# A convolution by matmul transforms beside a gated MLP: block-diagonal transforms of 128 rows replaced by pairs of dense 64-row matmul tiles

## The chip, the cores and the metric

One core of one Trainium2 chip runs the whole program. The metric is device time in microseconds (us) for one execution. Times quoted are medians of several executions. Most executions of one kernel agree within about 1%. Engine names in the profile: PE is TensorE (matmuls), PEld its weight loads, DVE is VectorE, ACT is ScalarE, SP issues the transfers (DMA).

## The reference, cut to what matters

Three parts are added: the input, a long convolution of a gated sequence done through a Fourier transform, and a gated MLP ("gate/up" and "down" below). Inputs have 2048 positions and 640 channels, the MLP has 1728 hidden columns, all in bf16.

```python
def reference(A_q, A_k, A_v, A_shift_k, A_ssm_k, A_ssm_D, B_x, B_w_gate, B_w_up, B_w_down):
    def _A_ref(q, k, v, shift_k, ssm_k, ssm_D):
        B, S, D = q.shape
        ks = shift_k.shape[-1]
        k_pad = jnp.pad(k, ((0, 0), (ks - 1, 0), (0, 0)))
        k_shift = jnp.zeros_like(k)
        for t in range(ks):
            k_shift = k_shift + k_pad[:, t:t + S, :] * shift_k[:, ks - 1 - t][None, None, :]
        kv = k_shift * v
        L = 2 * S
        kv_pad = jnp.pad(kv, ((0, 0), (0, S), (0, 0)))
        kf_pad = jnp.pad(ssm_k, ((0, 0), (0, S)))
        kv_f = (lambda x, axes=(-2,-1): jnp.fft.rfft2(x.astype(jnp.float32), axes=axes))(kv_pad[:, None, :, :], axes=(1, 2))
        kf_f = (lambda x, axes=(-2,-1): jnp.fft.rfft2(x.astype(jnp.float32), axes=axes))(kf_pad[:, None, :], axes=(1, 2))
        kf_f = (lambda x, *d: x.transpose(*d))(kf_f, 1, 2, 0)
        y_f = kv_f * kf_f[None, :, :, :]
        y = (lambda x, s, axes=(-2,-1): jnp.fft.irfft2(x, s=s, axes=axes).astype(jnp.bfloat16))(y_f, (1, L), axes=(1, 2))[:, 0, :S, :]
        y = y + kv * ssm_D[None, None, :]
        return q * y

    def _B_ref(x, w_gate, w_up, w_down):
        g = jnp.einsum("bsd,df->bsf", x, w_gate)
        u = jnp.einsum("bsd,df->bsf", x, w_up)
        h = _sigmoid(g) * u
        return jnp.einsum("bsf,fd->bsd", h, w_down)

    x = A_q
    xn = _layernorm(x, axis=-1)
    return x + _A_ref(xn, A_k, A_v, A_shift_k, A_ssm_k, A_ssm_D) + _B_ref(xn, B_w_gate, B_w_up, B_w_down)
```

## The kernel before

The kernel does the transforms as matmuls. 640 channels are cut into 10 steps of 64. Each step goes through:

- the first transform (`rec_st1`): data is the stationary operand, the table `F` moves; the result T goes to SBUF by ScalarE;
- the second transform (`rec_st2`): table `M` is stationary, T moves; the result is the spectrum S (real and imaginary part, of the gated sequence and of the filter);
- the complex product on VectorE (`rec_prod`) gives Z;
- the third and fourth transform go back.

The tables of the first two are block-diagonal: 128 rows hold two independent problems of 64 rows, so half of what TensorE multiplies is zero. (The third's table is padded in the same way.) ScalarE builds the padded table `Mb` from a dense one at the start (`load_M`).

All operations are recorded with priorities and planned durations; a small list scheduler inside the program then fixes the order of instructions on each engine. Gate/up and down matmuls fill TensorE between the steps of the convolution. The constants `GA, GB, CA, CB` set those priorities. Tags such as "c" and "g" are buffer pools: "c" has 3 PSUM banks for transforms, "g" has 5 for the MLP.

```python
    def load_M(pri):
        b = "Mc"

        def view():
            return tl[b][:, 0:K1 * 2 * K2].bitcast(F16).rearrange("p (k s m) -> p k s m", s=2, m=K2)
        for i in range(2):
            ks = slice(16 * i, 16 * i + 16)
            dma(lambda ks=ks: nc.sync.dma_start(view()[:, ks].bitcast(U16), Mdram.ap()[:, ks]), 512, 4096,
                w=[(b, i)], alloc=[(b, "V")] if i == 0 else (), pri=pri)
        for i in range(4):
            ks = slice(8 * i, 8 * i + 8)
            for p in range(2):
                cs = slice(p * K2, (p + 1) * K2)
                m, mn = Wm[:, p:p + 1], Wm[:, 2 + p:3 + p]
                act(1024 + 200, lambda ks=ks, cs=cs, m=m: nc.scalar.activation(
                    Mb[:, ks, 0:2, cs], view()[:, ks], ACT.Copy, scale=m),
                    r=[(b, i // 2), ("W",)], w=[("M", i, p, 0)], pri=pri + 24)
                act(512 + 200, lambda ks=ks, cs=cs, mn=mn: nc.scalar.activation(
                    Mb[:, ks, 2, cs], view()[:, ks, 1], ACT.Copy, scale=mn),
                    r=[(b, i // 2), ("W",)], w=[("M", i, p, 1)], pri=pri + 24)

    # ... (loads, shift and gating of k and v)

    def rec_st1(idx, pri, dp):
        half, sub = divmod(idx, NSUB)
        j0 = sub * JS
        part = 0 if j0 < HPART[0][1] else 1
        hb = f"ht{half}{part}"
        hj = j0 - HPART[part][0]
        hr = [(hb, g, p) for g in range(G) for p in range(2)]
        T = f"T{idx}"
        for j in range(JS):
            c = f"c1_{idx}_{j}"

            def f(j=j, c=c):
                pt = tl[c].rearrange("p (x n) -> p x n", x=2)
                nc.tensor.matmul(pt[:, 0, :], lhsT=tl[f"kvt{idx}"][:, :, :, j].rearrange("p b n -> p (b n)"),
                                 rhs=Fb[:], start=True, stop=True)
                nc.tensor.matmul(pt[:, 1, :], lhsT=tl[hb][:, hj + j, :, :].rearrange("p b n -> p (b n)"),
                                 rhs=Fb[:], start=True, stop=True)
            pe(2 * mm(256), f, r=[(f"kvt{idx}",), ("F",)] + hr + ([(T, "a")] if j else []),
               w=[(c,)] + ([] if j else [(T, "a")]), alloc=[(c, "c")] + ([] if j else [(T, "T")]), pri=pri + dp * j / JS)
            act(512, lambda j=j, c=c: nc.scalar.copy(out=tl[T][:, :, j, :],
                                                     in_=tl[c].rearrange("p (x n) -> p x n", x=2)),
                r=[(c,)], w=[(T, j)], pri=pri + dp * j / JS)

    def rec_st2(idx, pri, dp):
        T, S_ = f"T{idx}", f"S{idx}"
        for kb8 in range(K1 // 8):
            for im in range(2):
                c = f"c2_{idx}_{kb8}_{im}"

                def f(kb8=kb8, im=im, c=c):
                    Tv = tl[T].rearrange("p x j (k r g) -> p (x j) k r g", r=2, g=G)
                    pp = tl[c].rearrange("p (k n) -> p k n", k=8)
                    for kk in range(8):
                        k = 8 * kb8 + kk
                        nc.tensor.matmul(pp[:, kk, :], lhsT=Mb[:, k, 0, :], rhs=Tv[:, :, k, im, :],
                                         start=True, stop=False)
                        nc.tensor.matmul(pp[:, kk, :], lhsT=Mb[:, k, 1 + im, :], rhs=Tv[:, :, k, 1 - im, :],
                                         start=False, stop=True)

                def ev(kb8=kb8, im=im, c=c):
                    dst = tl[S_][:, im].rearrange("p x (j k g) -> p k x j g", k=K1, g=G)
                    for_in = tl[c].rearrange("p (k x g) -> p k x g", k=8, g=G)
                    nc.scalar.copy(out=dst.rearrange("p k x j g -> p k (x j) g")[:, 8 * kb8:8 * kb8 + 8], in_=for_in)
                q = pri + dp * (2 * kb8 + im) / 8
                z = (kb8, im) == (0, 0)
                pe(16 * mm(64), f, r=[(T, j) for j in range(JS)] + ([] if z else [(S_, "a")]) +
                   [("M", kb8, p, e) for p in range(2) for e in range(2)],
                   w=[(c,)] + ([(S_, "a")] if z else []), alloc=[(c, "c")] + ([(S_, "S")] if z else []), pri=q)
                act(512, ev, r=[(c,)], w=[(S_, im)], pri=q)

    def rec_prod(idx, pri):
        S_, Z = f"S{idx}", f"Z{idx}"
        n = JS * K1 * G

        def X(im):
            return tl[S_][:, im, 0, :]

        def H(im):
            return tl[S_][:, im, 1, :]

        def tv(b):
            return tl[b].rearrange("p n b j -> p (n b j)")

        sr = [(S_, 0), (S_, 1)]
        for o, (a, b, cc, d, al) in enumerate(((0, 0, 1, 1, ALU.subtract), (0, 1, 1, 0, ALU.add))):
            t = f"tp{idx}_{o}"
            dve(n, 2, lambda o=o, a=a, b=b: nc.vector.tensor_tensor(tl[Z][:, o], X(a), H(b), ALU.mult),
                r=sr, w=[(Z, o)], alloc=[(Z, "Z")] if o == 0 else (), pri=pri)
            dve(n, 2, lambda t=t, cc=cc, d=d: nc.vector.tensor_tensor(tv(t), X(cc), H(d), ALU.mult),
                r=sr, w=[(t,)], alloc=[(t, "t")], pri=pri)
            dve(n, 2, lambda t=t, o=o, al=al: nc.vector.tensor_tensor(tl[Z][:, o], tl[Z][:, o], tv(t), al),
                r=[(t,)], w=[(Z, o)], pri=pri)
```

## Time and profile before

| | before |
|---|---|
| median of 3 runs, us | 303.77 (302.59 to 306.47) |
| span of the profiled execution, us | 300.3 |
| PE / DVE / ACT busy | 93% / 63% / 59% |
| second transform: matmuls, distance of starts | 1280 of 64 columns, 29 ns |
| first transform: matmuls, distance of starts | 160 of 256 columns, 109 ns |

The first lines of the page of the kernel before. In the slices each digit is one fortieth of the span, in tenths busy; PEclk is the granted TensorE clock in tenths.

```profile
span 300.3 us, 7199 instructions
...
PE 278.7 (93%) x2957; PEld 184.7 (62%) x2957; DVE 188.6 (63%) x414; ACT 176.4 (59%) x364; POOL 0.7 (0%) x6
...
PE   8793999799999599999999999999998999999993
...
ACT  1551289979898398768467678796964534510000
...
PEclk9998699999999999999999999999999999999998
```

PE is nearly full over most of the span. Its largest holes are at the left, and PEclk drops (6) just after the deepest.

Two windows of the kernel before; the columns are busy us of PE, PEld, DVE, ACT and POOL, then granted clock, DMA share and GB/s.

```profile
20.00:40.00 20.00, 14.86 (x67) 6.47 (x66) 8.67 (x15) 6.27 (x11) 0.00 (x0) 0.83 1.04 170
40.00:60.00 20.00, 17.72 (x87) 8.48 (x85) 19.59 (x52) 19.46 (x31) 0.00 (x0) 1.00 1.03 285
```

Between 40 and 60 us ACT is busy 19.5 of 20 us, and PE only 17.7. The weight loads of the second transform, in the groups of instructions (count, busy us, mean ns):

```profile
L531 PEld LDWEIGHTS <-Mb 128*128 128x128 f16 x640 | 40.5, 97 | 1.9
...
L412 ACT ACTIVATE Mb<-V_389,Wm 128x1024 f16<-128x1024 f16 x8 | 9.2, 1148 | 0.0
...
L415 ACT ACTIVATE Mb<-V_389,Wm 128x512 f16<-128x512 f16 x8 | 5.8, 722 | 0.0
```

The table takes ACT 9.2 + 5.8 = 15.0 us. The second transform, in order of time; the columns are start, duration, engine, line:

```profile
61.66 0.38 PE L689 MATMUL g_669<-xnT_177,w_601 128*128 128x512 bf16 x1
...
61.88 0.19 PE L531 MATMUL c_678<-T_530,Mb 128*128 128x64 bf16 x1
61.88 0.10 PEld L533 LDWEIGHTS <-Mb 128*128 128x128 f16 x1
61.91 0.19 PE L533 MATMUL c_678<-T_530,Mb 128*128 128x64 bf16 x1
...
61.94 0.19 PE L531 MATMUL c_678<-T_530,Mb 128*128 128x64 bf16 x1
...
61.97 0.20 PE L533 MATMUL c_678<-T_530,Mb 128*128 128x64 bf16 x1
```

The matmuls start 29 to 30 ns apart, though each lasts 190 ns: they are pipelined, so busy time per matmul says little and the distance of starts is what counts. Each has its own weight load of about 97 ns, which also runs at that pace. The first matmul of the group follows the last gate/up matmul after 0.22 us, which is just that matmul's own 512 columns. So TensorE is the bound, and the second transform fills 1280 x 29 ns = 37 us of it, the first 160 x 109 ns = 17.5 us.

What TensorE waited for, longest first (the list of waits; total us, times, longest):

```profile
PE c_356 L445 <- DMA kt_164<-in_A_k_dram: 5.1, 1, 5.1
PE g_1473 L689 <- DMA w_1324<-in_B_w_up_dram: 3.2, 1, 3.2
...
PE c_3920 L586 <- DVE Z_3879 L567: 1.2, 1, 1.2
```

### The profile page before, as it was taken

To read this page: it belongs to the slowest core of one execution; us is meant where nothing else is said; L and a number is where in the kernel's file an instruction comes from. 1 tells how busy PE (TensorE), PEld (TensorE's weight loads), DVE (VectorE), ACT (ScalarE), POOL (GpSimd) and SP (SyncE) were. 2 spreads that over 40 slices of the span, in tenths; PEclk is the share of its full clock that TensorE was granted. 3 is DMA by queue.
4 is the path that set the end of the run, shared out by engine and by line. 5 is a ranking of instruction groups with operands and counts; after the bars stand their busy time and mean duration, and the time that the engine had idled before them with its cause. 6 is when DMAs were issued, how large, how long until landed. Compare 5 with 4: busy or idle time off the path is not lost.

```text
span 300.3 us, 7199 instructions
## 1 busy us (share of the span) xinstructions
PE 278.7 (93%) x2957; PEld 184.7 (62%) x2957; DVE 188.6 (63%) x414; ACT 176.4 (59%) x364; POOL 0.7 (0%) x6
## 2 busy tenths in 40 slices
PE   8793999799999599999999999999998999999993
PEld 3351345376767287887787786667664545567772
DVE  6971599999965599978325244433599372236531
ACT  1551289979898398768467678796964534510000
POOL 0000000000000000000000000000000000000000
PEclk9998699999999999999999999999999999999998
DMA  7899899933599900850388604871909499659411
GB/s 231 223 155 139 154 315 370 183 35 75 114 148 148 201 2 3 127 156 2 106 203 207 122 0 78 156 203 41 160 24 196 130 267 262 140 101 203 169 46 44
DMA packets 135688, 42.33 MB, mean 141 GB/s; under 512 B 109736, under 2 KB 131304, under 8 KB 135656
## 3 DMA queue, kind: packets, MB, share of 16 engines
q1 hardware_dynamic: 135656, 41.88, 66.2%
q8 instruction: 23, 0.38, 0.6%
q14 instruction: 9, 0.07, 0.1%
HBM read 36.62 MB, written 5.24 MB: 139 GB/s over the span
## 4 chain that ended last, share of the span: by engine, by line
PE 61%; DVE 13%; DMA 13%; SPq 8%; issue 3%; ACT 0%; DVEq 0%; ACTq 0%
SPq L442 3%; DMA kt_164<-in_A_k_dram 2%; DMA At<-dftA 2%; DMA w_1324<-in_B_w_up_dram 2%; SPq L743 2%; SPq L440 2%; DMA kt_3465<-in_A_q_dram 2%; DMA B_2337<-dftB 1%; DMA B_4063<-dftB 1%; DMA yd<-yt_2464 1%; DMA B_2695<-dftB 1%; DVE kt_3465 L748 1%; DVE hT_83 L704 1%; DVE st_540 L645 1%; DVE hT_82 L704 1%
## 5 line engine op out<-in xcount | busy, mean ns | idle before, releaser
L531 PEld LDWEIGHTS <-Mb 128*128 128x128 f16 x640 | 40.5, 97 | 1.9
L533 PEld LDWEIGHTS <-Mb 128*128 128x128 f16 x640 | 39.3, 97 | 1.9
L717 PEld LDWEIGHTS <-hT_82 128*128 128x128 bf16 x224 | 21.5, 98 | 7.8
L717 PEld LDWEIGHTS <-hT_83 128*128 128x128 bf16 x224 | 21.4, 98 | 7.6
L779 PE MATMUL g_89<-sig_85,ident 128*128 128x512 bf16 x31 | 8.4, 439 | 1.4 <-POOL ident masks.py:199 1.4
L412 ACT ACTIVATE Mb<-V_389,Wm 128x1024 f16<-128x1024 f16 x8 | 9.2, 1148 | 0.0
L689 PEld LDWEIGHTS <-w_97 128*128 128x128 bf16 x40 | 4.3, 109 | 6.8 <-issue 3.5
L689 PEld LDWEIGHTS <-w_427 128*128 128x128 bf16 x40 | 3.9, 97 | 5.8 <-issue 2.0
L779 PEld LDWEIGHTS <-ident 128*128 128x128 bf16 x31 | 3.4, 111 | 5.9 <-issue 2.1
L689 PEld LDWEIGHTS <-w_401 128*128 128x128 bf16 x40 | 3.8, 98 | 5.1 <-DMA w_401<-in_B_w_up_dram 0.5
L689 PEld LDWEIGHTS <-w_158 128*128 128x128 bf16 x40 | 3.9, 100 | 4.6 <-issue 0.6
L689 PEld LDWEIGHTS <-w_1324 128*128 128x128 bf16 x30 | 2.7, 97 | 6.3 <-DMA w_1324<-in_B_w_up_dram 3.7
L563 DVE TENSOR_TENSOR Z_2985<-S_2763 128x1024 bf16<-128x1024 bf16 x2 | 1.4, 688 | 8.2 <-ACT S_2763 L539 8.2
L689 PEld LDWEIGHTS <-w_3845 128*128 128x128 bf16 x40 | 3.7, 98 | 4.0
L689 PEld LDWEIGHTS <-w_3556 128*128 128x128 bf16 x40 | 3.8, 98 | 3.8
L672 ACT COPY xnT_177<-g_176 128x640 bf16<-128x640 bf16 x1 | 0.7, 693 | 8.9 <-PE g_176 L669 8.9
L689 PEld LDWEIGHTS <-w_4034 128*128 128x128 bf16 x40 | 3.6, 98 | 3.5
L415 ACT ACTIVATE Mb<-V_389,Wm 128x512 f16<-128x512 f16 x8 | 5.8, 722 | 0.0
L689 PEld LDWEIGHTS <-w_935 128*128 128x128 bf16 x40 | 3.8, 98 | 3.0
L689 PEld LDWEIGHTS <-w_601 128*128 128x128 bf16 x40 | 3.7, 97 | 3.2
L689 PEld LDWEIGHTS <-w_2088 128*128 128x128 bf16 x40 | 3.7, 98 | 2.9
L689 PEld LDWEIGHTS <-w_3268 128*128 128x128 bf16 x40 | 3.6, 97 | 2.9
(1275 smaller groups left out, 918.5 us busy)
## 6 DMA issues: line engine op xcount, KB each, us to landing
out_dram<-acc SPq DMA_DIRECT2D x8, 320.0 KB, 2.6
acc<-in_A_q_dram SPq DMA_DIRECT2D x3, 640.0 KB, 6.3
wd<-in_B_w_down_dram SPq DMA_DIRECT2D x3, 480.0 KB, 7.8
kt_164<-in_A_k_dram SPq DMA_DIRECT2D x4, 320.0 KB, 7.2
vt_170<-in_A_v_dram SPq DMA_DIRECT2D x4, 320.0 KB, 7.2
kt_1144<-in_A_k_dram SPq DMA_DIRECT2D x4, 320.0 KB, 7.1
vt_1231<-in_A_v_dram SPq DMA_DIRECT2D x4, 320.0 KB, 7.6
vt_3066<-yd SPq DMA_DIRECT2D x16, 80.0 KB, 2.7
```

Source lines behind the costliest of these rows:

```text
L412: act(1024 + 200, lambda ks=ks, cs=cs, m=m: nc.scalar.activation(Mb[:, ks, 0:2, cs], view()[:, ks], ACT.Copy, scale=m), r=[(b, i // 2), (" ...
L415: act(512 + 200, lambda ks=ks, cs=cs, mn=mn: nc.scalar.activation(Mb[:, ks, 2, cs], view()[:, ks, 1], ACT.Copy, scale=mn), r=[(b, i // 2), ...
L440: dma(lambda c0=c0, r0=r0: nc.sync.dma_start(ktv(half)[r0:r0 + N1, 3:3 + N2, :], k3[:, :, c0:c0 + HALF]), 320, 160, w=[(kb, g)], alloc=[(k ...
L442: dma(lambda c0=c0, r0=r0: nc.sync.dma_start(vtv(half)[r0:r0 + N1, :, :], v3[:, :, c0:c0 + HALF]), 320, 160, w=[(vb, g)], alloc=[(vb, "vt" ...
L531: nc.tensor.matmul(pp[:, kk, :], lhsT=Mb[:, k, 0, :], rhs=Tv[:, :, k, im, :], start=True, stop=False)
L533: nc.tensor.matmul(pp[:, kk, :], lhsT=Mb[:, k, 1 + im, :], rhs=Tv[:, :, k, 1 - im, :], start=False, stop=True)
L645: dve(320, 1, lambda i=i, s2=s2: nc.vector.bn_stats(stat(i, s2), acc[:, 4 * tr + i, s2 * 320:(s2 + 1) * 320]), r=[("acc", 4 * tr + i)], w= ...
L689: nc.tensor.matmul(tl[c][:], lhsT=tl[wb][:, k, o:o + P], rhs=tl[X][:, k, :], start=(k == 0), stop=(k == NC - 1))
L704: dve(512, 1, lambda c=c: nc.vector.tensor_tensor(hT[:, fc, :], tl[sg][:], tl[c][:], ALU.mult), r=[(c,), (sg,)], w=[(hk, fc)], pri=pri)
L717: nc.tensor.matmul(tl[pd[i]][:, 0:320], lhsT=hT[:, fc, t4 * P:(t4 + 1) * P], rhs=wd[:, fc, 320 * i:320 * i + 320], start=(fc == 0), stop=( ...
L743: dma(lambda qs=qs, g=g: nc.sync.dma_start(xv()[:, qs, g, :], xs[:, g, qs, cs]), 160, 160, w=[(xb, j) for j in range(8 * i, 8 * i + 8)], a ...
L779: plan.op("PE", 0.3, lambda: nc.tensor.matmul(tl["wps"][:], lhsT=ident[:], rhs=tl["warm"][:], start=True, stop=True), r=[("warm",)], w=[(" ...
```

## The change

The intent is to stop multiplying zeros. A 64-row matmul uses the upper or the lower half of the array's rows. The idea is that two of them, on different halves, run side by side. So:

- `F` and `M` become dense. Every full-row matmul of the first two transforms becomes a pair of 64-row ones, each with half the useful width, into separate PSUM banks;
- the second transform puts the real part on partitions 0 to 63 and the imaginary part on 64 to 127. The product then needs S with its halves exchanged: two transfers of 256 KB per step do that. In exchange the product is two VectorE operations of 2048 elements in place of six of 1024. Its additions do not vanish: they move into the third transform, whose table loses its zeros and takes the signs (320 matmuls of 128 columns in place of 160 of 256, the same columns in all);
- the dense `M` is loaded whole (1.5 MB instead of 1 MB) and ScalarE no longer builds a table;
- the pools become 4 and 4 banks, as pairs need them, and the scheduler's constants were set anew.

```diff
# the tables
-    M = np.zeros((2, N2, K1, 2, K2))
-    M[:, :, :, 0, :] = np.cos(th)[None]
-    M[:, :, :, 1, :] = np.sin(th)[None]
-    M = M.reshape(P, K1, 2, K2)
+    M = np.zeros((2, N2, K1, 3, K2))
+    M[:, :, :, 0, :] = np.sin(th)[None]
+    M[:, :, :, 1, :] = np.cos(th)[None]
+    M[:, :, :, 2, :] = -np.sin(th)[None]
+    M = M.reshape(P, K1, 3 * K2)
# ... (the first table likewise for two groups of channels; masks removed)
# sizes and constants
-    GA, GB = 25.0, 125.0
-    CA, CB = 35.0, 205.0
+    GA, GB = 25.0, 140.0
+    CA, CB = 35.0, 215.0
-   ... "c": 3, "g": 5}
+   ... "c": 4, "g": 4}
# ... (load_M: 16 ScalarE operations removed, table loaded dense, 1.5 MB)
+    def mm2(i, out, lhs, rhs, start, stop):
+        for h in range(2):
+            rs = slice(64 * h, 64 * h + 64)
+            nc.tensor.matmul(out[h], lhsT=lhs[rs], rhs=rhs[rs], start=start, stop=stop)
+
# rec_st1
-        for j in range(JS):
-            c = f"c1_{idx}_{j}"
-
-            def f(j=j, c=c):
-                pt = tl[c].rearrange("p (x n) -> p x n", x=2)
-                nc.tensor.matmul(pt[:, 0, :], lhsT=tl[f"kvt{idx}"][:, :, :, j].rearrange("p b n -> p (b n)"),
-                                 rhs=Fb[:], start=True, stop=True)
-                nc.tensor.matmul(pt[:, 1, :], lhsT=tl[hb][:, hj + j, :, :].rearrange("p b n -> p (b n)"),
-                                 rhs=Fb[:], start=True, stop=True)
-            pe(2 * mm(256), f, r=[(f"kvt{idx}",), ("F",)] + hr + ([(T, "a")] if j else []),
-               w=[(c,)] + ([] if j else [(T, "a")]), alloc=[(c, "c")] + ([] if j else [(T, "T")]), pri=pri + dp * j / JS)
-            act(512, lambda j=j, c=c: nc.scalar.copy(out=tl[T][:, :, j, :],
-                                                     in_=tl[c].rearrange("p (x n) -> p x n", x=2)),
-                r=[(c,)], w=[(T, j)], pri=pri + dp * j / JS)
+        for u in range(2 * JS // 4):
+            x, jq = u % 2, 4 * (u // 2)
+            cs = [f"c1_{idx}_{u}_{h}" for h in range(2)]
+
+            def f(x=x, jq=jq, cs=cs):
+                pt = [tl[c].rearrange("p (j n) -> p j n", j=4) for c in cs]
+                for j in range(4):
+                    if x == 0:
+                        lhs = tl[f"kvt{idx}"][:, :, :, jq + j].rearrange("p b n -> p (b n)")
+                    else:
+                        lhs = tl[hb][:, hj + jq + j, :, :].rearrange("p b n -> p (b n)")
+                    mm2(j, [q[:, j, :] for q in pt], lhs, Fb, True, True)
+            q = pri + dp * u / 4
+            pe(4 * mm(128), f, r=[("F",)] + ([(f"kvt{idx}",)] if x == 0 else hr) + ([(T, "a")] if u else []),
+               w=[(c,) for c in cs] + ([] if u else [(T, "a")]),
+               alloc=[(c, "c") for c in cs] + ([] if u else [(T, "T")]), pri=q)
+            for h in range(2):
+                act(512, lambda x=x, jq=jq, h=h, c=cs[h]: nc.scalar.copy(
+                    out=tl[T][:, x, jq:jq + 4, :, 2 * h:2 * h + 2],
+                    in_=tl[c].rearrange("p (j k g) -> p j k g", j=4, g=2)),
+                    r=[(cs[h],)], w=[(T, u, h)], pri=q)
 
     def rec_st2(idx, pri, dp):
         T, S_ = f"T{idx}", f"S{idx}"
         for kb8 in range(K1 // 8):
-            for im in range(2):
-                c = f"c2_{idx}_{kb8}_{im}"
-
-                def f(kb8=kb8, im=im, c=c):
-                    Tv = tl[T].rearrange("p x j (k r g) -> p (x j) k r g", r=2, g=G)
-                    pp = tl[c].rearrange("p (k n) -> p k n", k=8)
-                    for kk in range(8):
-                        k = 8 * kb8 + kk
-                        nc.tensor.matmul(pp[:, kk, :], lhsT=Mb[:, k, 0, :], rhs=Tv[:, :, k, im, :],
-                                         start=True, stop=False)
-                        nc.tensor.matmul(pp[:, kk, :], lhsT=Mb[:, k, 1 + im, :], rhs=Tv[:, :, k, 1 - im, :],
-                                         start=False, stop=True)
-
-                def ev(kb8=kb8, im=im, c=c):
-                    dst = tl[S_][:, im].rearrange("p x (j k g) -> p k x j g", k=K1, g=G)
-                    for_in = tl[c].rearrange("p (k x g) -> p k x g", k=8, g=G)
-                    nc.scalar.copy(out=dst.rearrange("p k x j g -> p k (x j) g")[:, 8 * kb8:8 * kb8 + 8], in_=for_in)
-                q = pri + dp * (2 * kb8 + im) / 8
-                z = (kb8, im) == (0, 0)
-                pe(16 * mm(64), f, r=[(T, j) for j in range(JS)] + ([] if z else [(S_, "a")]) +
-                   [("M", kb8, p, e) for p in range(2) for e in range(2)],
-                   w=[(c,)] + ([(S_, "a")] if z else []), alloc=[(c, "c")] + ([(S_, "S")] if z else []), pri=q)
-                act(512, ev, r=[(c,)], w=[(S_, im)], pri=q)
+            cs = [f"c2_{idx}_{kb8}_{b}" for b in range(2)]
+
+            def f(kb8=kb8, cs=cs):
+                Tv = tl[T].rearrange("p x j (k r) g -> p (x j) k r g", r=2)
+                pp = [tl[c].rearrange("p (k n) -> p k n", k=8) for c in cs]
+                for kk in range(8):
+                    k = 8 * kb8 + kk
+                    o = [q[:, kk, :] for q in pp]
+                    mm2(kk, o, Mb[:, k, K2:3 * K2], Tv[:, :, k, 0, :], True, False)
+                    mm2(kk, o, Mb[:, k, 0:2 * K2], Tv[:, :, k, 1, :], False, True)
+            q = pri + dp * kb8 / 4
+            z = kb8 == 0
+            pe(16 * mm(64), f, r=[(T, u, h) for u in range(4) for h in range(2)] + ([] if z else [(S_, "a")]) +
+               [("M", kb8 // 2)], w=[(c,) for c in cs] + ([(S_, "a")] if z else []),
+               alloc=[(c, "c") for c in cs] + ([(S_, "S")] if z else []), pri=q)
+            for b in range(2):
+                act(512, lambda b=b, kb8=kb8, c=cs[b]: nc.scalar.copy(
+                    out=tl[S_][:, b, 0:2].rearrange("p x (j k g) -> p k (x j) g", k=K1, g=G)[:, 8 * kb8:8 * kb8 + 8],
+                    in_=tl[c].rearrange("p (k n g) -> p k n g", k=8, g=G)),
+                    r=[(cs[b],)], w=[(S_, b, 0)], pri=q)
 
     def rec_prod(idx, pri):
         S_, Z = f"S{idx}", f"Z{idx}"
-        n = JS * K1 * G
-
-        def X(im):
-            return tl[S_][:, im, 0, :]
-
-        def H(im):
-            return tl[S_][:, im, 1, :]
-
-        def tv(b):
-            return tl[b].rearrange("p n b j -> p (n b j)")
-
-        sr = [(S_, 0), (S_, 1)]
-        for o, (a, b, cc, d, al) in enumerate(((0, 0, 1, 1, ALU.subtract), (0, 1, 1, 0, ALU.add))):
-            t = f"tp{idx}_{o}"
-            dve(n, 2, lambda o=o, a=a, b=b: nc.vector.tensor_tensor(tl[Z][:, o], X(a), H(b), ALU.mult),
-                r=sr, w=[(Z, o)], alloc=[(Z, "Z")] if o == 0 else (), pri=pri)
-            dve(n, 2, lambda t=t, cc=cc, d=d: nc.vector.tensor_tensor(tv(t), X(cc), H(d), ALU.mult),
-                r=sr, w=[(t,)], alloc=[(t, "t")], pri=pri)
-            dve(n, 2, lambda t=t, o=o, al=al: nc.vector.tensor_tensor(tl[Z][:, o], tl[Z][:, o], tv(t), al),
-                r=[(t,)], w=[(Z, o)], pri=pri)
+        for h in range(2):
+            o, i = slice(64 * h, 64 * h + 64), slice(64 - 64 * h, 128 - 64 * h)
+            dma(lambda o=o, i=i: nc.sync.dma_start(tl[S_][o, :, 2, :], tl[S_][i, :, 1, :]), 256, 2048,
+                r=[(S_, 0, 0), (S_, 1, 0)], w=[(S_, 2, h)], pri=pri - 4)
+        for b in range(2):
+            dve(2 * JS * P, 2, lambda b=b: nc.vector.tensor_tensor(
+                tl[Z][:, b], tl[S_][:, b, 0:1, :].to_broadcast((P, 2, JS * P)), tl[S_][:, b, 1:3, :], ALU.mult),
+                r=[(S_, b, 0), (S_, 2, 0), (S_, 2, 1)], w=[(Z, b)], alloc=[(Z, "Z")] if b == 0 else (), pri=pri)
 
# ... (rec_st3: eight evictions of 256 columns become four of 512; gate and up allocated together;
#      the scheduler's costs of transfers; one more dependence of the down projection)
```

## The prediction

> **What bounds the kernel now.** TensorE. The page has PE busy 278.7 us of a 300.3 us span (93%), DVE 63%, ACT 59%. The table of ten-microsecond windows shows PE nearly full from 110 us on. Its idle time is mainly in the first 60 us (49 of 60 busy): the DMA share is about 1.0, k, v and filter loads land late, ACT builds the padded table (8 x 1148 + 8 x 722 ns = 15.0 us).
>
> From the starts of matmuls in the timeline, array time is: gate/up 117 us, down 61, first transform 17.6 (160 matmuls of 256 columns, 109 ns apart), second transform 37.9 (1280 of 64 columns, 29 ns apart), third 17.5. Together the changed two hold 55 us.
>
> **What the change does.**
> 1. Half-row matmuls in pairs. If a pair runs together, the first transform needs 160 pairs of 128 columns, estimate 56 ns each = 9 us (saves 8.6); the second 640 pairs of 64 columns, 29 ns = 18.7 us (saves 19). But the second keeps 1280 matmuls, each with its weight load. The Trainium skill ("TensorE: Matmul & The Clock Gate", section "Wait — 56ns, not 53.3ns?") says that starts never come closer than about 25 ns, however small the matmul; this kernel is already at 29. No trace here shows pairs. I expect 45 to 50 ns a pair: 6 us saved there, about 14 us in both.
> 2. Some 63 blocks of half-row matmuls stand among full ones: 126 switches. The skill ("TensorEngine Tiling (Array Packing)", section "Key Properties") says that a change of mode drains the engine. Not in this trace; a 64-column matmul lasts 190 ns against a 29 ns pace, so a drain could cost 160 ns. I reckon 60 ns: 7 us lost.
> 3. ACT loses the table's 15 us and, with eight 410 ns evictions made four of about 600 ns per step, another 9 us. The first step starts earlier: 3 us, though the table's DMA grows from 1 to 1.5 MB.
> 4. DVE loses 60 products of 690 ns (41 us), gets 20 of about 1300 ns (26 us). Off the path.
> 5. New wait: ten swaps of 2 x 256 KB through the load queue, estimate 4 to 5 us to landing (256 KB loads of table B took 2.7 to 4.7). Product chain per step: before 4.1 us, after 7 us. PE's order has about 7 us of other matmuls there; 4 us of stalls in total.
> 6. Two PSUM pairs in place of five free slots for gate/up; eviction of a pair costs ACT 1.2 us: 2 us of stalls.
>
> Sum: -14 + 7 - 3 + 4 + 2 = -4, and -17 if pairs fully overlap; weighing both, about -10.
>
> **Prediction:** 293 us, 8 in 10 within 280 to 307; faster by over 2% 0.57, within 2% 0.27, slower 0.16.
>
> **What would show it.** Step 1: spacing of starts in the second transform (29 or about 48 ns a pair). Step 2: the gap between the last full matmul and the first half-row one, and back. Step 3: the first second-transform matmul before 61.9 us. Step 5: PE idle before the third transform, released by DVE, and the swap's time to landing. PE busy should fall to 255 to 270 us.
>
> **What would make it wrong.** Full overlap with free switching (280 or less); drains of 200 ns, or weight loads that no longer hide (above 305); swaps queued behind weight and k/v loads, so that the single S buffer holds up every step.

## The result, and the profile after

| | before | after |
|---|---|---|
| median, us | 304.62 (4 runs) | 285.67 (284.85 to 286.67, 4 runs) |
| ratio | | 0.938 (95%: 0.931 to 0.946), faster |
| span of the profiled execution, us | 300.3 | 283.1 |
| start of the first second-transform matmul, us | 61.9 | 53.6 |
| start of the last third-transform matmul, us | 233.6 | 230.9 |
| last gate/up matmul, us | 264.7 | 243.0 |

A ratio here and below is the mean time of one kernel's fast runs over that of the other's in the same rounds, so it is not quite the ratio of the two medians. Executions over 1.5% slower than the fastest of the same kernel are left out of the means.

The page of the kernel after, the same lines:

```profile
span 283.1 us, 7793 instructions
...
PE 266.2 (94%) x3277; PEld 158.9 (56%) x3277; DVE 175.0 (62%) x374; ACT 160.7 (57%) x308; POOL 0.7 (0%) x6
...
PE   8799659999999999999999999999999999799993
...
ACT  1444232777979697686345688778888454312000
...
PEclk9999989999999999999999999999999999999999
```

PE stays the bound (94%), and the slices between the head and the end are nearly all 9. The first windows:

```profile
20.00:40.00 20.00, 14.18 (x89) 6.84 (x88) 11.62 (x20) 6.79 (x13) 0.00 (x0) 1.00 1.18 181
40.00:60.00 20.00, 20.00 (x221) 9.33 (x220) 17.77 (x46) 11.34 (x23) 0.00 (x0) 0.92 0.95 292
```

ACT now has 11.3 of 20 us between 40 and 60 us, and PE is full there. The hole from 20 to 40 us stays. The weight loads of the second transform are now of 64 x 128:

```profile
L480 PEld LDWEIGHTS <-Mt 64*128 64x128 f16 x1280 | 20.6, 93 | 10.1 <-issue 9.2
```

The pairs, in order of time. Both matmuls of a pair start at once on the clock of this print, and the next pair follows 30 to 40 ns later:

```profile
84.47 0.23 PEld L480 LDWEIGHTS <-Mt 64*128 64x128 f16 x12
84.48 0.20 PE L480 MATMUL c_1303<-T_1158,Mt 64*128 64x64 bf16 x1
84.48 0.20 PE L480 MATMUL c_1304<-T_1158,Mt 64*128 64x64 bf16 x1
84.52 0.19 PE L480 MATMUL c_1303<-T_1158,Mt 64*128 64x64 bf16 x1
84.52 0.19 PE L480 MATMUL c_1304<-T_1158,Mt 64*128 64x64 bf16 x1
84.55 0.19 PE L480 MATMUL c_1303<-T_1158,Mt 64*128 64x64 bf16 x1
84.55 0.19 PE L480 MATMUL c_1304<-T_1158,Mt 64*128 64x64 bf16 x1
```

Over the whole trace the 1247 distances between neighbouring starts inside second-transform blocks sum to 18.3 us, 14.7 ns a matmul or 29 ns a pair. Two of a pair start 3 to 4 ns apart. So the pairs overlap completely.

A change of tiling, the last gate/up matmuls and the first half-row pair:

```profile
76.25 0.81 PE L666 MATMUL g_1145<-xnT_277,w_728 128*128 128x512 bf16 x3
...
76.99 0.17 PEld L480 LDWEIGHTS <-ht_668 64*128 64x128 bf16 x6 [0.42 <-DVE t_1178 L469]
77.00 0.23 PE L480 MATMUL c_1182<-Ft,ht_668 64*128 64x128 f16 x1
77.00 0.23 PE L480 MATMUL c_1183<-Ft,ht_668 64*128 64x128 f16 x1
77.06 0.22 PE L480 MATMUL c_1182<-Ft,ht_668 64*128 64x128 f16 x1
```

The three gate/up matmuls start at 76.25, 76.47 and 76.69. The next would follow after 0.22 us; the half-row pair starts after 0.31 us, at 77.00, and its weight load only just before it, at 76.99, instead of a matmul ahead. (The bracket puts an idle time of 0.42 us before the weight load down to VectorE; but at 133 of the 134 changes, whatever released them, the weight load starts at most 5 ns before its matmul, where it goes 214 ns ahead between matmuls of 512 columns. The spare matmuls below test this further.) Of the 67 changes to half rows, 45 look like this one: 311 to 312 ns where 216 are needed by 512 columns (96 ns lost). Those after 320, 128 or 80 columns lose 95 to 98 ns. On the way back, 121 to 125 ns pass after a 64-column pair in place of 29 (93 ns lost).

What TensorE waited for after:

```profile
PE c_428 L480 <- DVE kvt_423 L473: 3.0, 1, 3.0
PE c_368 L425 <- DMA kt_161<-in_A_k_dram: 2.8, 1, 2.8
PE g_4496 L695 <- DVE hT_82 L682: 2.0, 1, 2.0
```

None of these is a product or a swap; the longest wait for a product is 0.2 us. The swaps' transfers, in the list of issues (count, KB each, us from issue to landing):

```profile
S_597<-S_597 SPq DMA_DIRECT2D x2, 256.0 KB, 3.8
...
S_1305<-S_1305 SPq DMA_DIRECT2D x2, 256.0 KB, 5.3
S_1656<-S_1656 SPq DMA_DIRECT2D x2, 256.0 KB, 3.3
```

**A ledger of the span.** I summed, in both traces, the distances between neighbouring matmul starts. What a matmul's own columns need is work: columns / 2.4 in ns, plus 4 ns, a fit to the paces in these traces (512 columns every 216 ns, 256 every 109, 128 every 56, 64 every 29). Remainders of 10 ns or less count as work too; up to 95 ns at each change of tiling is switching; the rest is idle.

| us | before | after | difference |
|---|---|---|---|
| idle between matmuls | 23.1 | 18.5 | -4.6 |
| switching (134 changes after) | 0 | 12.5 | +12.5 |
| work, and the two ends of the span | 277.2 | 252.1 | -25.1 |
| span | 300.3 | 283.1 | -17.2 |

The convolution's own chain of steps hardly got shorter (its end moved by 2.7 us). The gain came out in the gate/up matmuls, which moved into the TensorE time that the transforms left free, and were done 22 us earlier.

### The profile page after: what moved, and what is told of

It reads as the page before. It is cut to its first block, busy times and chain, and to the rows that moved or that the text cites. A ratio compares the mean times of both kernels' runs of the same rounds, so it can differ in the third digit from the quotient of the medians.

```text
span 283.1 us, 7793 instructions
## 1 busy us (share of the span) xinstructions
PE 266.2 (94%) x3277; PEld 158.9 (56%) x3277; DVE 175.0 (62%) x374; ACT 160.7 (57%) x308; POOL 0.7 (0%) x6
## 4 chain that ended last, share of the span: by engine, by line
PE 55%; DMA 18%; SPq 12%; DVE 8%; ACT 2%; issue 2%; ACTq 0%; DVEq 0%
SPq L422 4%; DMA kt_1341<-in_A_k_dram 3%; SPq L420 3%; DMA kt_161<-in_A_k_dram 2%; DMA acc<-in_A_q_dram 2%; DMA S_2559<-S_2559 2%; SPq L733 2%; DMA B_2553<-dftB 2%; DMA yd<-yt_4576 2%; DMA S_2030<-S_2030 1%; DMA kt_4147<-in_A_q_dram 1%; DVE acc L747 1%; DMA yd<-yt_4681 1%; SPq L585 1%; SPq L540 1%
## 5 line engine op out<-in xcount | busy, mean ns | idle before, releaser
L695 PEld LDWEIGHTS <-hT_81 128*128 128x128 bf16 x224 | 20.8, 98 | 10.0 <-issue 2.2
L480 PEld LDWEIGHTS <-Mt 64*128 64x128 f16 x1280 | 20.6, 93 | 10.1 <-issue 9.2
L695 PEld LDWEIGHTS <-hT_82 128*128 128x128 bf16 x224 | 21.3, 98 | 8.1
L758 PE MATMUL g_88<-sig_84,ident 128*128 128x512 bf16 x31 | 9.0, 462 | 1.4 <-POOL ident masks.py:199 1.4
L666 PEld LDWEIGHTS <-w_404 128*128 128x128 bf16 x40 | 4.2, 109 | 5.6 <-issue 2.3
L666 PEld LDWEIGHTS <-w_96 128*128 128x128 bf16 x40 | 3.9, 98 | 5.8 <-issue 1.4
L666 PEld LDWEIGHTS <-w_3911 128*128 128x128 bf16 x40 | 3.8, 98 | 4.0
L666 PEld LDWEIGHTS <-w_154 128*128 128x128 bf16 x40 | 3.8, 98 | 3.8
L666 PEld LDWEIGHTS <-w_728 128*128 128x128 bf16 x40 | 3.6, 98 | 4.1
L666 PEld LDWEIGHTS <-w_3609 128*128 128x128 bf16 x40 | 3.6, 97 | 4.0
L695 PE MATMUL g_4496<-wd,hT_81 128*128 128x320 bf16 x14 | 3.9, 299 | 2.0 <-DVE hT_82 L682 2.0
L666 PEld LDWEIGHTS <-w_462 128*128 128x128 bf16 x40 | 3.4, 98 | 3.8
L666 PEld LDWEIGHTS <-w_3305 128*128 128x128 bf16 x40 | 3.3, 98 | 3.6
L666 PEld LDWEIGHTS <-w_3019 128*128 128x128 bf16 x40 | 3.4, 98 | 3.5
L666 PEld LDWEIGHTS <-w_2164 128*128 128x128 bf16 x40 | 3.5, 98 | 3.3
L666 PEld LDWEIGHTS <-w_2402 128*128 128x128 bf16 x40 | 3.3, 97 | 3.3
L666 PEld LDWEIGHTS <-w_848 128*128 128x128 bf16 x40 | 3.3, 98 | 3.3
L666 PEld LDWEIGHTS <-w_1267 128*128 128x128 bf16 x30 | 2.8, 98 | 3.0
L622 DVE BATCH_NORM_STATS2 st_108<-acc 128x6 f32<-128x320 bf16 x8 | 3.4, 466 | 1.7 <-DMA acc<-in_A_q_dram 1.7
L666 PEld LDWEIGHTS <-w_4183 128*128 128x128 bf16 x30 | 2.7, 98 | 2.6
```

The lines of the kernel that those rows point to most:

```text
L480: nc.tensor.matmul(out[h], lhsT=lhs[rs], rhs=rhs[rs], start=start, stop=stop)
L622: dve(320, 1, lambda i=i, s2=s2: nc.vector.bn_stats(stat(i, s2), acc[:, 4 * tr + i, s2 * 320:(s2 + 1) * 320]), r=[("acc", 4 * tr + i)], w= ...
L666: nc.tensor.matmul(tl[c][:], lhsT=tl[wb][:, k, o:o + P], rhs=tl[X][:, k, :], start=(k == 0), stop=(k == NC - 1))
L695: nc.tensor.matmul(tl[pd[i]][:, 0:320], lhsT=hT[:, fc, t4 * P:(t4 + 1) * P], rhs=wd[:, fc, 320 * i:320 * i + 320], start=(fc == 0), stop=( ...
L758: plan.op("PE", 0.3, lambda: nc.tensor.matmul(tl["wps"][:], lhsT=ident[:], rhs=tl["warm"][:], start=True, stop=True), r=[("warm",)], w=[(" ...
```

## The experiments

Theory A: the gain is overlap of the pairs on a TensorE that is the bound, less the price of the switches. Rival B: the gain is ScalarE freed of the table, and the new order of instructions. The kernel before ran again beside each group; the medians are 304.6 us with the result and 304.0, 304.4 and 302.5 with the three groups of experiments (the third on another chip). So the groups may be set side by side to about 2 us. The changed kernel was not run again: "after" below is always 285.67. Medians here are of the fast runs alone.

| run | median, us | ratio to before |
|---|---|---|
| after | 285.67 | 0.938 |
| halves apart (e1) | 298.11 | 0.979 |
| upper half only (e1) | 312.96 | 1.028 |
| first transform full-row (e2) | 288.97 | 0.951 |
| spare full-row matmuls (e3) | 295.81 | 0.972 |
| spare half-row pairs (e3) | 286.04 | 0.940 |
| table work, old order (e4) | 295.39 | 0.970 |
| table work, planned (e4) | 296.64 | 0.980 |
| no swap (e5) | 284.21 | 0.934 |
| before with after's scheduling (e6) | 300.42 | 0.989 |
| groups merged, both (e7) | 311.0 | 1.027 |
| merged, first transform | 298.48 | 0.983 |
| merged, second transform | 302.41 | 0.998 |

### Is it the overlap? Halves apart

```diff
-                for kk in range(8):
-                    mm2(...)     # upper half, lower half, upper half, ...
+                for h in range(2):
+                    for kk in range(8):
+                        mm1(h, ...)   # all of one half, then all of the other
```

> The changed kernel with one edit: within each block all matmuls of the upper 64 rows come first, then all of the lower 64, so no two neighbours can run side by side. Same matmuls, same blocks, same switches, same program order of everything else. Theory A (the gain is the overlap of pairs on a TensorE that is the bound): the second transform goes from 29 ns a pair to 29 ns a matmul (+18 us), the first from 56 ns a pair to 56 or more a matmul (+9 us), and the time rises by nearly all of it: 306 to 314 us, no faster than the kernel before. Rival B (the gain is ScalarE freed of the table and a better order of instructions): 286 to 291 us.

Measured 298.11 us: 12.4 more than after, half of what was expected. The experiment did not do what I meant. In its trace (start, duration, count of a run of matmuls):

```profile
73.20 1.77 PE L479 MATMUL c<-T,Mt 64*128 64x64 bf16 x64
```

64 matmuls that end after 1.77 us, the last of which lasts 0.19, start every 25 ns on average, and not every 29. Around the change from one half to the other, single starts fit two streams running at once: the old half keeps its 29 ns pace for three more starts, and three starts of the new half (8, 48 and 83 ns into the change) lie between them. The trace does not name the half, so this is read from the distances. The first transform, with runs of only four per half, kept its full overlap (its neighbour distances sum to 9.2 us against 8.8 after). Only the second got slower, by 14.1 us of summed distances, and nearly nine tenths of that (12.4 us) showed in the time. So the design was wrong, but the numbers fit A.

### Upper half only

```diff
         for h in range(2):
-            rs = slice(64 * h, 64 * h + 64)
+            rs = slice(0, 64)
             nc.tensor.matmul(out[h], lhsT=lhs[rs], rhs=rhs[rs], start=start, stop=stop)
```

> The changed kernel with both matmuls of every pair on rows 0 to 63 (wrong result on purpose): same matmuls, blocks and switches in the same order, but no two can run side by side. It repairs the run with halves apart, where short runs of one half still overlapped the other. Theory A (the gain is overlap on a TensorE that is the bound): second transform 29 ns a matmul (+18 us), first 56 ns (+9 us); by the last run nearly nine tenths of added TensorE time showed in the time, so 305 to 314 us, which is no faster than before. Rival B (ScalarE's table, schedule): under 295 us.

Measured 312.96 us, 27.3 more than after and 2.8% slower than before. (Its result is wrong by design, though it stayed within the tolerance of the comparison with the reference.) One of its blocks:

```profile
92.53 2.06 PE L480 MATMUL c<-T,Mt 64*128 64x64 bf16 x64
```

64 starts in 2.06 - 0.19 = 1.87 us, 29.7 ns each: no overlap left. The distances inside the blocks sum to 37.2 us in the second transform (18.3 after) and 18.1 in the first (8.8 after): 28.2 us more, of which 27.3 show in the time. With everything else of the change in place, the pairs without overlap are slower than the kernel before. The overlap is therefore necessary for the gain, and B alone is refuted.

### The first transform back to full rows

```diff
-    (pairs of 128 columns, 40 groups in half-row blocks)
+    (the kernel before's first transform: 160 matmuls of 256 columns on the padded F)
```

> The changed kernel with the first transform put back to full-row matmuls of 256 columns on the zero-padded table; the second transform stays in pairs. Theory A with a switch of tiling costing about 94 ns each way (read in the trace after): TensorE loses 8 us of overlap and wins back 33 of the 67 half-row blocks, 33 x 188 ns = 6 us, so 287 to 290 us. If switches were free it would be 294; if only the number of blocks mattered it would be under 284.

Measured 288.97 us as the median of three runs (287.7 to 291.76), inside the range; a fourth run was slow (292.83). The scheduler laid the program out anew here, so a few microseconds may be its doing. Taken as it is, pairing the first transform is worth about 3 us. By the trace its overlap saves about 8 us of TensorE work, and the 66 changes of tiling that it brings take 6 us of that back, since its blocks are short.

### The price of a switch

```diff
                 for kk in range(8):
+                    if kk == 4:   # overwritten later by the matmul that belongs there
+                        nc.tensor.matmul(pp[0][:, 7, :], lhsT=Mb[:, k, 0:P], rhs=Tv[:, :, k, 0, :], start=True, stop=True)
```

The twin puts a half-row pair there instead.

> The changed kernel with one spare full-row matmul of 64 columns in the middle of each of the 40 second-transform groups (its result is overwritten, so the output stays right): 40 more switches each way. Theory (a switch costs 94 ns each way and TensorE is the bound): 40 x (188 + 29) = 8.7 us more, 293 to 296 us, against the twin with half-row spares. Rival (the gap at a switch only hides a wait that would be there anyway): within 2 us of the twin.

> The twin: the spare work is a half-row pair of 64 columns, which needs no switch. 40 x 29 ns = 1.2 us more: 286 to 288 us. The difference to the run with full-row spares is the price of 80 switches.

Measured 295.81 and 286.04 us. The difference, 9.8 us for 80 switches, is 122 ns each. In the trace a spare matmul and its neighbours (count 1 is the spare):

```profile
86.95 0.41 PE L480 MATMUL c<-T,Mt 64*128 64x64 bf16 x16
87.30 0.20 PE L524 MATMUL c<-T,Mt 128*128 128x64 bf16 x1
87.43 0.41 PE L480 MATMUL c<-T,Mt 64*128 64x64 bf16 x16
```

The last of the first 16 ends at 87.36 and so starts near 87.17; the spare comes 0.12 to 0.13 us later, and the next half-row matmul 0.13 us after the spare. Over all 40, the median distances are 121 and 135 ns, where 29 each would do: 92 and 106 ns lost, 7.9 us of the 9.8. A switch costs time on a bound engine, at about the price read off the trace, and the 134 switches of the change give back 12.5 us (by the trace) to 16 us (134 x 122 ns).

### ScalarE's table work put back

```diff
+        for i in range(4):
+            for p in range(2):
+                (ScalarE copies 128x1024 and 128x512 from the table into a spare buffer)
```

First with the old order of instructions kept, then with the work known to the scheduler.

> The changed kernel with ScalarE's 15 us of table work put back as sixteen copies of the old sizes, at the place where they stood before (among the first step's evictions), nothing waiting for them by name, all other instructions in the same order. Theory A: ScalarE is not the bound, but these hold up the first step; that moves TensorE's slack: 286 to 290 us. Rival B (the freed table work is the gain): 295 us or more.

> ScalarE's 15 us of table work put back again, but now with its duration told to the program's own scheduler, which lays gate/up matmuls around it as the kernel before had them, and with the second transform waiting for it as it did before. The earlier run with the old order cost about 10 us, which sat near the mark of rival B. Theory A (that run's loss came from a TensorE order made for a free ScalarE): 286 to 291 us. Rival B (the freed ScalarE time itself is worth 10 us): 294 us or more.

Measured 295.39 and 296.64 us: 9.7 and 11.0 more than after. This is where theory A fell short: I had allowed at most 5, and both runs reach the mark that I had set for B. The window of the first of these runs (to compare with 40 to 60 us above), and what was waited for from 40 to 62 us:

```profile
40.00:60.00 20.00, 14.08 (x72) 6.00 (x76) 11.74 (x21) 16.86 (x27) 0.00 (x0) 0.80 0.83 264
```

```profile
DVE hT L696 <- ACT sig L693: 7.5, 2, 4.4
...
PE c L494 <- DVE ht L461: 5.0, 1, 5.0
```

ACT is busy 16.9 us instead of 11.3, PE 14.1 instead of 20, and the granted clock is lower. Sigmoids stand among the table work on ACT; VectorE waits 7.5 us for two of them; next in its order stands the operation that readies the filter (`ht`), and TensorE waits 5.0 us for it. The first second-transform matmul starts at 63.5 us (61.7 in the planned run) instead of 53.6. Part of the loss is clock: before its last matmul this run has 17.1 us at half rate, against 3.4 us after. By the longer distances of matmuls there I estimate 4 to 5 us of the 10.7 us by which the span grew. So the table's ScalarE work was not harmless because ACT was only 59% busy: it sat at the one place where the start of the convolution hangs on ACT.

### Without the swaps

```diff
-            dma(lambda o=o, i=i: nc.sync.dma_start(tl[S_][o, :, 2, :], tl[S_][i, :, 1, :]), ...)
+            dma(lambda: None, ...)
-                ... tl[S_][:, b, 1:3, :], ALU.mult)
+                ... tl[S_][:, b, 0:2, :], ALU.mult)
```

> The changed kernel without the twenty swap transfers; the product reads the unswapped spectrum (wrong result on purpose), order of everything else unchanged. My prediction had 4 us of stalls for the swaps: then 281 to 283 us. If the matmuls that stand there hide them: 284.5 to 286.5 us.

Measured 283.65 to 284.44 us in three runs, 1.5 us less than after by the medians. The swaps are nearly hidden. A fourth execution, the profiled one, took 924 us with PE busy 97% of it: its 512-column matmuls start 840 ns apart in place of 216, although the recorded clock is 1.0. I leave it out and have no explanation, and there is no fast profile of this run.

### The scheduling edits alone, on the kernel before

```diff
-    GA, GB = 25.0, 125.0          # and CA, CB; pools c 3, g 5; costs of transfers
+    GA, GB = 25.0, 140.0          # and CA, CB; pools c 4, g 4; gate and up allocated together
```

> The kernel before with all of the change's scheduling edits alone: the two pairs of priority constants, the costs that it reckons for transfers, four PSUM slots each for the two pools, gate and up allocated together, the down projection's extra dependence. Theory A: 300 to 308 us, within 2% of before. Rival B (the order is the gain): under 297 us.

Measured 300.42 us, ratio 0.989 (0.983 to 0.994): a little over 1%, some 3.5 us. The order is a small part of the gain. It does not bring the convolution's start forward: in this run the first second-transform matmul starts at 61.4 us (61.9 before, 53.6 after).

### Fewer switches by merging groups

```diff
-    (one group per operation: 2 PSUM banks, 67 half-row blocks in the program)
+    (two groups per operation: 4 PSUM banks; 40, 52 or 48 blocks)
```

> An attempt to beat the changed kernel: two groups of the first transform, and two of the second, are made one operation with all four PSUM slots, so that 40 half-row blocks stand in the program instead of 67. 27 x 188 ns = 5 us less TensorE time: 280 to 283 us if the scheduler fills the longer evictions with gate/up and down matmuls, 286 or more if these run out and TensorE waits for ScalarE.

> Only the first transform's groups merged: 52 half-row blocks, 15 x 188 ns = 2.8 us less: 282 to 285 us.

> Only the second transform's groups merged: 48 half-row blocks, 19 x 188 ns = 3.6 us less: 281 to 284 us.

Measured 311.0, 298.48 and 302.41 us: all three slower than after, by far more than the switches are worth. From the trace of the run with both merged, its waits and the window in which the largest falls:

```profile
DVE Z L549 <- DMA S<-S: 9.8, 6, 3.4
...
PE c L569 <- DVE Z L549: 5.8, 3, 4.0
```

```profile
90.00:100.00 10.00, 6.35 (x101) 5.04 (x103) 3.05 (x3) 3.53 (x7) 0.00 (x0) 0.66 1.03 160
```

VectorE waits for a swap that was issued at 85.5 us, just behind a strided k load, and begins the product at 92.4. TensorE waits 4.0 us for the product, and then the clock is halved: the third-transform matmuls of 128 columns start 107 ns apart in that window, where 55 to 56 are normal. The run has 13.7 us at half rate before its last matmul, against 3.4 us after; that is at most 6.8 us lost, against 1.7. (Its mean granted clock of 0.948 says more than that, but 20.2 us at half rate lie behind the last matmul, where they cost no matmul time.) The larger loss is at the end, in the slices of its page:

```profile
PE   8797689999968779999999999999899999999000
```

The last matmul ends at 285.3 us, 6.8 us later than after (278.5), but then the program runs on for 22.4 us, against 4.6 after. So 17.8 of the 24.6 us by which the span grew lie behind the last matmul. The third transform ends at 259.4 us (231.2 after), 14 us behind the start of the last gate/up matmul (245.5). The convolution's last results are stored, read back and added when no matmul is left beside them. The other two runs show the same: 11.5 and 15.2 us behind the last matmul, and 5.6 and 3.8 us of TensorE waits for products. The switching in the ledger did fall as forecast, from 12.5 us to 7.5, 9.7 and 9.0. So no version that I made beats the changed kernel, and merging fails not for the switches: the convolution's chain falls behind, and its end stands alone. What put it behind was not separated by a run; the swap's wait, met with less other work in between, may be one part.

## Why the prediction was right, point by point

The time lay in the range (285.67 in 280 to 307), on the fast side, and "faster" was the likeliest class. The size was low: about 10 us were forecast, 19 came. Part of the hit is luck. The sum weighed two branches, -4 with 45 to 50 ns a pair, which I expected, and -17 with full overlap, which happened. And -17 is close to -19 only because errors offset each other: the switches cost 5 to 9 us more than reckoned, and the freed table and the swaps came out better. The terms of the sum:

1. **Overlap, -14 forecast, -25 in the trace and 27.3 us by experiment.** The step that failed is "I expect 45 to 50 ns a pair". It is 29. I took the floor of about 25 ns between starts from the Trainium skill ("TensorE: Matmul & The Clock Gate", section "Wait — 56ns, not 53.3ns?") and applied it to pairs. The same page, section "The mechanism", says that tiles on different row groups start about 4 ns apart; the trace agrees, with 3 to 4 ns. The floor does not hold across two tiles here; whether it holds for one was not tested (upper half only ran at 29.7 ns).
2. **Switches, +7 forecast, +12.5 measured.** The count was right (67 blocks for 63). "I reckon 60 ns" was too little: 93 to 98 ns in the trace, 122 by experiment.
3. **Freed ScalarE, -3 forecast.** "The first step starts earlier: 3 us": it started 8.3 us earlier, and putting the work back into the changed kernel costs 10 to 11 us, lost clock included. The fewer evictions of the third transform (80 of 431 ns became 40 of 600) were not tested alone. Mis-sized threefold, and I should have seen it: the windows before show ACT at 19.5 of 20 us just where PE has a hole.
4. **VectorE off the path.** It is at 62% after, and the six products of 0.69 us became two of 1.22 us. In the kernel before, TensorE's waits for products came to 1.2 us in all. Nothing contradicts the step; no run tested it alone.
5. **Swaps, +4 forecast, about 1.5 measured.** Landing took 3.3 to 5.3 us, as estimated. "About 7 us of other matmuls" there hid it. What I named as a danger, swaps queued behind k loads, shows only in the trace of the merged version.
6. **PSUM slots, +2 forecast.** Not tested alone; the scheduling edits together, these included, gain 3.5 us on the kernel before.

The terms do not add up by themselves. Removing the overlap costs 27.3 us, and restoring the table 10 more; with the scheduling's 3.5 and 12.5 to 16 for the switches given back, that would put the kernel before at 310 to 315 us, and it is at 304.6. In the ledger the two kernels differ by only 4.6 us of idle time, so the table seems to have cost the kernel before less than it costs the changed one. Perhaps its order fitted the table better; what removing the table alone does to the kernel before was not run, and this stays open.

## What to carry to other kernels

When the matmul engine is the bound and a table is block-diagonal, try pairs of 64-row matmuls. Here they gave the full factor of two even at 64 columns, but every change to half rows or back cost about 0.1 us, so count the blocks and not only the matmuls. Look for a busy helper engine in the windows where the bound engine has holes, and not at its share of the whole span. Before you regroup work to save such small costs, check which chain will end last: in the merged version the matmuls ended 6.8 us later, but 22 us of stores, loads and additions came behind them.

## What the Trainium skill lacked or had wrong

- "TensorE: Matmul & The Clock Gate", section "Wait — 56ns, not 53.3ns?": the floor of about 25 ns between starts is stated without a limit, although section "The mechanism" of the same page has about 4 ns between row groups. For half-row pairs the starts are 3 to 4 ns apart, and 14.7 ns on average over 1247 distances, each matmul with its own weight load.
- "TensorEngine Tiling (Array Packing)", section "Key Properties": says that changing the mode drains the engine, but no price. Here 93 to 98 ns each way in the trace, 122 ns by the twin runs; at 133 of 134 changes the next weight load starts at most 5 ns before its matmul.
- "TensorE: Matmul & The Clock Gate", section "The mechanism": its list says that weight loads overlap running matmuls only when the row group differs, while the paragraph above it also lets a load into the background weight buffer go ahead. The trace of the kernel before agrees with the paragraph and not with the list: full-row weight loads of 97 ns ran at a pace of 29 ns under full-row matmuls of 190 ns. The list also has matmuls start strictly in program order. With halves apart, three starts of the second half seem to lie among the last ones of the first half (read from the distances; the trace does not name the half, so this is not shown).
- The same page, section "What's actually happening", has the half-rate clock after an idle window of about 3.4 us. The traces agree in part. After 4.0 us of waiting in the merged run, 128-column matmuls started 107 ns apart in place of 55 to 56. But a distance of 2.2 us between matmul starts came before half rate with the table work put back (at 253.4 us, half rate from 256.8), and one of 3.5 us in the kernel before (at 97.7 us) brought none.
